# Moving the first fold of d K into the backward convolutions, and changing three loads, in an S4-gated SSM layer's forward and backward pass

## The chip, the cores and the metric

The kernel runs on one core of one Trainium2 chip. The metric is the device time in microseconds of one execution, from its first to its last instruction with what lies around them; lower is better. Five executions of the kernel before took 730.01, 740.09, 734.91, 728.99 and 732.19 us, so its median is 732.19 us.

## The reference, cut to what matters

The reference computes one layer and, by `jax.vjp`, its eleven gradients. All tensors are bf16; there are 2048 rows (time) of 512 channels, 128 states per channel, and a feed-forward network of width 1792.

```
xn  = layernorm(x)
K   = Re sum_n C[d,n] dB[d,n] exp(dt[d] A[d,n])**l       # the kernel of the convolution, per channel d
s   = causal convolution of xn with K along time + xn * Dskip
g   = silu( silu(xn @ w1) @ w2 )
out = x + s * g
and the gradients of out for x, A, B, C (real and imaginary), log_dt, Dskip, w1, w2
```

The backward pass first forms the gradient of `s` and of the network's output. The convolutions are done as Fourier transforms, so going back through them gives, per channel block, the gradient of xn through the convolution (dU) and the gradient of K (d K). From d K come the gradients of A, B, C and log_dt; "fold" is the first step on that way, which sums d K over groups of time steps. The gradient of x comes last, out of dU, the network's share and the layer norm.

## The kernel before, in words

Channels are cut into four blocks of 128, called b = 0 to 3; time rows are cut into eight chunks of two 128-row tiles, called c = 0 to 7. The parts of the work are Python generators that issue some instructions and then yield; helpers named `paced`, `woven` and `interleave` take turns among them. What comes out of that is not yet the order on the engines: the framework's scheduler arranges the issued instructions on each engine's queue when the kernel is built, with waits on semaphores between them. So the order on an engine is fixed at build time and can be read from the built kernel, and an instruction can stand before work that was issued earlier in the source.

The last part of `tile_recurrent_scan...` (L1132 to L1147) is the backward pass. Its stages:

1. **Backward convolutions**, about 300 to 465 us in the trace. `gen_conv_bwd` (L637) takes each block b through `forward(b)` (transform of the output gradient, lines L286, L297, L298, with its transposing DMAs L288) and `rest(b)`: a complex product on VectorE (L330 to L335), an inverse transform to d K (L310, then L319, cast by ScalarE at L44 and stored at L664), a second complex product, a second inverse transform to dU (L672, stored at L674). Beside it, at 1.8 steps to one, run `gen_ffn_da` (L867; matmuls L893 into ps_da and L904 into ps_dx, ScalarE's Silu and Tanh at L882 and L883, VectorE's L895) and `gen_out` (L607). `gen_out` makes the output: it loads rows of s, of the network's output (go_g) and of x (go_x, L626, one buffer), multiplies (L629), adds (L630) and stores with GpSimd's queue (L631). The load of x for a chunk is issued at the start of that chunk's own step.
2. **State gradients beside the rest of the network**, about 465 to 540 us. `gen_ssm_bwd` (L825) begins with six transposing loads of parameters (L346), then `ssm_fold` for b = 0: four loads of d K into the tile GE (L687), 23 short matmuls into one PSUM tile G21 (L703 and L705; the trace calls it G), and two casts by ScalarE into Gf (L706). Then come transposing loads of a table, YT (L725), VectorE's products Gb (L714), matmuls ps_v of YT and Gb (L736), ScalarE's casts Vb, VectorE's products Tp (L746), and sums by matmul (L758 to L762). The work runs in 16 groups of eight columns (L830), four to a block; the next block's fold is issued at the third group of a block.
3. **State gradients, gradients of w2 and w1, layer norm**, about 540 us to the end: `gen_dw2` (L911), `gen_dw1` (L943) and `gen_ln_bwd` (L961) take turns with the rest of `gen_ssm_bwd`. The layer norm loads dU, the network's share and rows of grad_out (Gt, L974, two buffers) and stores at L996.

Most loads and stores go through SyncE's queue (SP); a few go through ScalarE's, and the output stores through GpSimd's. The PSUM pool `pc` has two buffers; the transforms (ps_s, ps_i), the fold (G21) and ps_v all take theirs from it. The PSUM pool `pf` has three; the network's matmuls use it.

Of the kernel before, what the change touches and what calls it, by code (L numbers as in the profile page):

```python
# [13 lines left out]
BF16 = mybir.dt.bfloat16  # L14
# [3 lines left out]
P = 128  # L18
# [1 line left out]
PB = 18  # L20


BR, SR = 1.8, 0.5

E_EXP = [256 * i for i in range(1, 9)] + list(range(8)) + [258, 260, 262, 516, 772]
Y_EXP = [8 * j for j in range(1, 8)] + [64, 128, 192]
NE = len(E_EXP)
# [579 lines left out]
def gen_out(k, pool):  # L607

    nc = k.nc
    TT = nc.vector.tensor_tensor  # L610
    n = k.T // 2
    rows = lambda ap: ap.rearrange("p t (b d) -> p b t d", b=4)

    def load(c):
        ts = slice(2 * c, 2 * c + 2)
        S = pool.tile([P, 4, 2, P], BF16, name="go_s", tag="go_s", bufs=2)
        nc.sync.dma_start(S[:].rearrange("p b t d -> p b (t d)"), k.Sd[:, :, 256 * c:256 * c + 256].rearrange("b p n -> p b n"))
        g = pool.tile([P, 2, k.D], BF16, name="go_g", tag="go_g", bufs=2)
        nc.sync.dma_start(g[:], k.Od[:, ts, :])
        return S, g  # L620
    q = [load(0), load(1)]
    yield
    for c in range(n):
        S, g = q.pop(0)
        x = pool.tile([P, 2, k.D], BF16, name="go_x", tag="go_x", bufs=1)
        nc.sync.dma_start(x[:], k.x_v[:, 2 * c:2 * c + 2, :])  # L626
        nc.scalar.activation(out=g[:], in_=g[:], func=ACT.Silu)
        yield
        TT(out=rows(g[:]), in0=rows(g[:]), in1=S[:], op=ALU.mult)  # L629
        TT(out=x[:], in0=x[:], in1=g[:], op=ALU.add)  # L630
        k.st(k.o0_v[:, 2 * c:2 * c + 2, :], x[:])  # L631
        if c + 2 < n:
            q.append(load(c + 2))
        yield
# [47 lines left out]
def ssm_fold(k, b, sb):  # L682

    nc, pc = k.nc, k.pc
    GE = sb.tile([P, 8, 8, 32], BF16, name="GE", tag="GE", bufs=1)
    for a in range(4):
        nc.sync.dma_start(GE[a:P:4].rearrange("p i t q -> p i (t q)"), k.dKd[b, a].rearrange("i j r -> j i r"))  # L687
    G21 = pc.tile([P, 2, 512], F32, name="G21", tag="pc")
    ID, SH, WR, MX = 0, 1, 2, 3
    z0 = [(ID, GE[:, 0, 0:8, :], (0, 8, 16)), (ID, GE[:, 1:8, 0, :], (0, 0, 7)), (ID, GE[:, 1:8, 1, :], (0, 0, 7)),  # L690
          (ID, GE[:, 2:8, 2, :], (0, 1, 7)), (ID, GE[:, 4:8, 3, :], (0, 3, 7))]
    for st, e0 in ((SH, 0), (WR, 1)):
        z0 += [(st, GE[:, 1:8, 7, :], (0, e0, e0 + 7)), (st, GE[:, 2:8, 6, :], (0, e0 + 1, e0 + 7)),
               (st, GE[:, 4:8, 5, :], (0, e0 + 3, e0 + 7))]
    z0 += [(MX, GE[:, 4:8, 4, :], (0, 3, 7)), (WR, GE[:, 4:8, 4, :], (0, 4, 8))]
    z1 = [(ID, GE[:, 1, 2, :], (1, 0, 1)), (ID, GE[:, 1, 6, :], (1, 2, 3))]
    for t in (3, 4, 5):
        z1 += [(ID, GE[:, 1, t, :], (1, 1, 2)), (ID, GE[:, 2:4, t, :], (1, 3, 5))]
    Gf = sb.tile([P, 32, NE, 4], BF16, name="Gf", tag="Gf", bufs=2)
    for bank, terms in ((0, z0), (1, z1)):  # L700
        n = 16 if bank == 0 else 5
        ov = G21[:, bank, 0:32 * n].rearrange("p (e q) -> p e q", e=n)
        nc.tensor.matmul(out=G21[:, bank, 0:32 * n], lhsT=k.zero[:], rhs=GE[:].rearrange("p i t q -> p (i t q)")[:, 0:32 * n], start=True, stop=False)  # L703
        for i, (st, src, (bk, e0, e1)) in enumerate(terms):
            nc.tensor.matmul(out=ov[:, e0:e1], lhsT=k.FO[:, st], rhs=src, start=False, stop=(i == len(terms) - 1))  # L705
        nc.scalar.copy(out=Gf[:, :, 16 * bank:16 * bank + n, :],  # L706
                       in_=G21[:, bank, 0:32 * n].rearrange("p (e q) -> p q e", e=n).unsqueeze(3).to_broadcast([P, 32, n, 4]))
    return Gf
# [116 lines left out]
def gen_ssm_bwd(k, sb):  # L825


    par = load_params(k, sb, 0, k.D)
    par["dt"] = k.dt[:]
    groups = [(b, h, q0) for b in range(4) for h in range(2) for q0 in (0, 8)]  # L830
    gf, half, yt, vb, tp, S, tail = {}, {}, {}, {}, {}, {}, []
    gf[0] = ssm_fold(k, 0, sb)
    yt[0] = ssm_turned(k, *groups[0], sb)
    yield
    n = len(groups)
    for i in range(n + 2):
        if i < n:
            b, h, q0 = groups[i]
            if q0 == 0:
                half[i // 2] = ssm_half(k, b, h, gf[b], sb)  # L840
            if i + 1 < n:
                yt[i + 1] = ssm_turned(k, *groups[i + 1], sb)
            vb[i] = ssm_v(k, q0, half[i // 2][0], yt.pop(i), sb)
            if (i % 4) == 2 and b < 3:
                gf[b + 1] = ssm_fold(k, b + 1, sb)
            yield
        if i >= 2:
            j = i - 2
            b, h, q0 = groups[j]
            if (j % 4) == 0:  # L850
                S[b] = sb.tile([P, 3, 32, 2, 4], F32, name="Sa", tag="Sa", bufs=2)
            ssm_sums(k, tp.pop(j), S[b][:, :, 16 * h + q0:16 * h + q0 + 8])
            yield
            if (j % 4) == 3:
                tail.append(gen_ssm_grads(k, b, S.pop(b), par, sb))
        if 1 <= i <= n:
            tp[i - 1] = ssm_products(k, groups[i - 1][2], vb.pop(i - 1), half[(i - 1) // 2][1], sb)
            yield
        if tail:
            if next(tail[0], "end") == "end":  # L860
                tail.pop(0)
    for t in tail:
        yield from t
# [97 lines left out]
def gen_ln_bwd(k, lw):  # L961
    nc = k.nc
    TT, STT = nc.vector.tensor_tensor, nc.vector.scalar_tensor_tensor
    D = k.D
    n = k.T // 2
    cols = lambda ap: ap.rearrange("p (b d) -> p b d", b=4)

    def load(c):
        du = lw.tile([P, 4, 2, P], BF16, name="du", tag="du", bufs=3)
        nc.sync.dma_start(du[:].rearrange("p b t d -> p b (t d)"), k.dUd[:, :, 256 * c:256 * c + 256].rearrange("b p n -> p b n"))  # L970
        pd = lw.tile([P, 2, D], BF16, name="pd_l", tag="pd_l", bufs=3)
        nc.sync.dma_start(pd[:], k.Pd[:, 2 * c:2 * c + 2, :])
        Gt = lw.tile([P, 2, D], BF16, name="Gt", tag="Gt", bufs=2)
        nc.sync.dma_start(Gt[:], k.g_v[:, 2 * c:2 * c + 2, :])  # L974
        return du, pd, Gt

    def sums(c, du, pd, Gt):

        m = lw.tile([P, 2, 4], F32, name="m", tag="m", bufs=2)
        for i in range(2):  # L980
            t = 2 * c + i
            jk = lw.tile([P, D], BF16, name="jk", tag="jk", bufs=1)
            STT(out=cols(pd[:, i]), in0=cols(pd[:, i]), scalar=1.0, in1=du[:, :, i, :], op0=ALU.mult, op1=ALU.add, accum_out=m[:, i, 0:1])
            STT(out=jk[:], in0=pd[:, i], scalar=1.0, in1=k.xn[:, t, :], op0=ALU.mult, op1=ALU.mult, accum_out=m[:, i, 1:2])
        STT(out=m[:, :, 2:4], in0=m[:, :, 0:2], scalar=-1.0 / D,
            in1=k.rstd[:, 2 * c:2 * c + 2].unsqueeze(2).to_broadcast([P, 2, 2]), op0=ALU.mult, op1=ALU.mult)
        for i in range(2):
            nc.scalar.activation(out=pd[:, i], in_=pd[:, i], func=ACT.Identity, scale=k.rstd[:, 2 * c + i:2 * c + i + 1], bias=m[:, i, 2:3])
        return pd, Gt, m

    def rows(c, pd, Gt, m):
        o1 = lw.tile([P, 2, D], BF16, name="o1", tag="o1", bufs=2)
        for i in range(2):
            STT(out=o1[:, i], in0=k.xn[:, 2 * c + i, :], scalar=m[:, i, 3:4], in1=Gt[:, i], op0=ALU.mult, op1=ALU.add)
        TT(out=o1[:], in0=o1[:], in1=pd[:], op=ALU.add)
        k.st(k.o1_v[:, 2 * c:2 * c + 2, :], o1[:])  # L996
    q, pend = [load(0)], None
    for c in range(n + 1):
        if c + 1 < n:
            q.append(load(c + 1))  # L1000
        yield
        cur = sums(c, *q.pop(0)) if c < n else None
        yield
        if pend:
            rows(c - 1, *pend)
        pend = cur


@with_exitstack
def kernel(ctx, tc, A_u, A_A_re, A_A_im, A_B_re, A_B_im, A_C_re, A_C_im, A_log_dt, A_Dskip, B_x, B_w1, B_w2, grad_out,  # L1010
           out_0, out_1, out_2, out_3, out_4, out_5, out_6, out_7, out_8, out_9, out_10, out_11):
    nc = tc.nc
    k = KCtx()
# [115 lines left out]
    base = dft_pool("dftb", es_x, {"cm2": 1, "xd": 1, "w8b": 2}, k.dft, side="right")  # L1129
    turn = itertools.cycle(["w8"] * 4 + ["w8b"] * 2)  # L1130
    k.dftb = SimpleNamespace(tile=lambda shape, dt, name, tag: base.tile(shape, dt, name=name, tag=next(turn) if tag == "w8" else tag))
    da = pool("da", es=es_d)  # L1132
    turned_in_place(k, k.W2, k.evw)
    bwd = gen_conv_bwd(k)
# [1 line left out]
    for i in range(4):  # L1136
        next(bwd)
    ffb = gen_ffn_da(k, da)
    paced(bwd, woven([ffb, out], [2, 1]), BR)
    es_x.close()  # L1140
    sb = pool("sb", side="right")
    ssm = gen_ssm_bwd(k, sb)
    paced(ffb, ssm, SR)
    run(out)
    es_d.close()
    fw = pool("fw")
    interleave([ssm, chained([gen_dw2(k, fw), gen_dw1(k, fw)]), after(8, gen_ln_bwd(k, fw))], [2, 1, 2])  # L1147
# [1 line left out]
_INS = ['A_u', 'A_A_re', 'A_A_im', 'A_B_re', 'A_B_im', 'A_C_re', 'A_C_im', 'A_log_dt', 'A_Dskip', 'B_x', 'B_w1', 'B_w2', 'grad_out']  # L1149
# [26 lines left out]
```

## Time and profile before

| what | value |
| --- | --- |
| median of five executions | 732.19 us (728.99 to 740.09) |
| the profiled execution: its own time | 730.01 us |
| its span, first to last instruction | 728.3 us |
| mean granted TensorE clock | 0.946 |
| TensorE (PE) busy, modelled | 594.1 us, 82% of the span |
| VectorE (DVE) busy | 553.4 us, 76% |
| ScalarE (ACT) busy | 495.8 us, 68% |
| GpSimd (POOL) busy | 100.0 us, 14% |
| HBM traffic | 65.14 MB read, 62.26 MB written |
| DMA queue of SP and the other hardware queue q1 | 135.29 MB, 70.6% of 16 engines' span |

The busy time of an engine is a sum over stages with different limits; the stages around the change have to be read one by one. In the timeline a row has the start in us, the duration in us, the engine, the line of the source, the operation and its tiles, and, where the engine sat idle just before, for how long and what ended it. SPq marks an instruction of SP's queue that only issues a transfer, with the time it took to issue. In the list of waits a row says who waited for whom, then the total in us, how many times, and the longest.

### The profile page before, as it was taken

The numbers are of one execution on the slowest core, as the hardware profiler recorded it, in microseconds if no ns is written. First come the engines' busy times: TensorE is split into PE (matmuls) and PEld (weight loads), VectorE is DVE, ScalarE is ACT, GpSimd is POOL, SyncE is SP. The second block draws the span as 40 slices with busy tenths as digits, with TensorE's granted clock in tenths as the row PEclk, the third lists the DMA queues.
The fourth block names the chain that finished last, engine by engine and source line by source line (L and its number), as shares of the span: only waits on it lengthen the run. The fifth ranks groups of instructions, "written<-read, shape, count | busy, mean of one in ns | idle before, by whom it ended". The sixth has DMA issues, their size and how long they took to land.

```text
span 728.3 us, 13901 instructions
## 1 busy us (share of the span) xinstructions
PE 594.1 (82%) x5459; PEld 427.1 (59%) x5500; DVE 553.4 (76%) x1070; ACT 495.8 (68%) x671; POOL 100.0 (14%) x180
## 2 busy tenths in 40 slices
PE   0677868869999965569798899978797979898895
PEld 0445646555665743346576576757576656566784
DVE  6969997969978759976895999756896898784100
ACT  6768858779889866858779687646755867661221
POOL 2172200000010026200000000000002103102300
PEclk9879998999999995879999999999999989999998
DMA  9867957769679986579987965589979999920772
GB/s 288 310 164 204 256 175 210 283 154 294 286 195 247 364 268 162 185 170 257 319 211 238 247 216 198 153 218 210 227 161 283 249 300 276 233 106 27 160 183 59
DMA packets 207043, 159.26 MB, mean 219 GB/s; under 512 B 129025, under 2 KB 185345, under 8 KB 203393
## 3 DMA queue, kind: packets, MB, share of 16 engines
q1 hardware_dynamic: 193856, 135.29, 70.6%
q0 software_dynamic: 6224, 18.10, 6.8%
q10 hardware_dynamic: 6896, 4.98, 2.2%
q8 instruction: 43, 0.70, 0.4%
q14 instruction: 24, 0.19, 0.1%
HBM read 65.14 MB, written 62.26 MB: 175 GB/s over the span
## 4 chain that ended last, share of the span: by engine, by line
issue 53%; POOL 5%; DVE 5%; DMA 2%; PE 0%; ACT 0%; POOLq 0%; ACTq 0%; SPq 0%; DVEq 0%
POOL out_dram L816 1%; POOL out_dram L939 1%; DMA out_dram<-o 1%; DVE YD L599 1%; DMA Gr<-in_grad_out_dram 1%; DMA Kd<-KE 1%; DVE sp_in L332 1%; POOL out_dram L631 1%; DVE ds L595 1%; POOL out_dram L996 1%; POOL out_dram L958 1%; DVE sp_in L337 0%; POOL g L598 0%; DVE YD L603 0%; DVE YD L601 0%
## 5 line engine op out<-in xcount | busy, mean ns | idle before, releaser
L44 ACT CAST dA<-ps_s 128x1024 bf16<-128x1024 f32 x96 | 94.6, 1041 | 17.0 <-PE ps_s L298 8.5
L310 PE MATMUL ps_i<-I,sp_in 128*128 128x256 bf16 x384 | 54.3, 288 | 15.6 <-ACT dK L44 7.5
L893 PE MATMUL ps_da<-doT,W 128*128 128x256 bf16 x448 | 61.9, 284 | 5.5 <-ACT doT L44 2.9
L541 PE MATMUL ps_h<-XT,W 128*128 128x256 bf16 x448 | 62.4, 290 | 1.5 <-ACT hT L44 0.8
L44 ACT CAST o<-ps_w 128x256 bf16<-128x256 f32 (+1 forms) x42 | 18.6, 442 | 57.1 <-PE ps_w L954 42.4
L558 PE MATMUL ps_o<-W,aT 128*128 128x512 bf16 x209 | 54.5, 393 | 3.3 <-ACT aT L549 2.0
L44 ACT CAST dB<-ps_i 128x1024 bf16<-128x1024 f32 x48 | 47.2, 1024 | 14.6 <-PE ps_i L310 12.2
L310 PEld LDWEIGHTS <-sp_in 128*128 128x128 bf16 x384 | 37.4, 102 | 31.3 <-DVE sp_in L333 11.9
L746 DVE TENSOR_TENSOR Tp<-Vb,Eb 128x1344 bf16<-128x1344 bf16 x64 | 52.4, 855 | 3.7 <-PE psS L762 3.6
L893 PEld LDWEIGHTS <-W 128*128 128x128 bf16 x448 | 44.9, 102 | 16.3 <-issue 6.7
L904 PE MATMUL ps_dx<-W,dhT 128*128 128x512 bf16 x224 | 53.7, 379 | 0.0
L541 PEld LDWEIGHTS <-W 128*128 128x128 bf16 x448 | 45.6, 104 | 12.6 <-issue 2.5
L936 PE MATMUL ps_w<-YD,a_tok 128*128 128x512 bf16 x210 | 50.8, 387 | 2.5 <-ACT o L44 1.6
L954 PE MATMUL ps_w<-dh_tok,xn 128*128 128x256 bf16 x448 | 50.5, 273 | 2.4 <-DMA dh_tok<-DHd 2.0
L895 DVE SCALAR_TENSOR_TENSOR dhT<-dhT,ps_da 128x512 bf16<-128x512 bf16 x56 | 37.5, 684 | 14.7 <-PE ps_da L893 14.5
L954 PEld LDWEIGHTS <-xn 128*128 128x128 bf16 x448 | 43.2, 98 | 8.5 <-issue 3.6
L44 ACT CAST Vb<-ps_v 128x672 bf16<-128x672 f32 x64 | 42.5, 723 | 7.6 <-PE ps_v L736 7.6
L286 PEld LDWEIGHTS <-TF 128*128 128x128 bf16 x384 | 26.0, 101 | 26.9 <-issue 15.4
L419 ACT ACTIVATE sn<-V 128x1024 bf16<-128x1024 int32 (+3 forms) x40 | 34.8, 887 | 8.8 <-DVE V L417 8.8
L297 PE MATMUL ps_s<-dB,F 128*128 128x512 bf16 x87 | 34.3, 401 | 6.3 <-DMA dB<-dA 3.8
L298 PE MATMUL ps_s<-dB,F 128*128 128x512 bf16 x95 | 36.6, 390 | 2.7 <-DMA dB<-dA 2.0
L447 PEld LDWEIGHTS <-YD 128*128 128x128 bf16 x512 | 24.0, 100 | 23.2 <-DVE YD L434 12.1
(220 smaller groups left out, 1363.6 us busy)
## 6 DMA issues: line engine op xcount, KB each, us to landing
Yd<-YD SPq DMA_DIRECT2D x8, 1024.0 KB, 6.3
sp_in<-Ud SPq DMA_DIRECT2D x8, 1024.0 KB, 7.2
h_in<-Hd SPq DMA_DIRECT2D x14, 512.0 KB, 5.5
Ed<-E SPq DMA_DIRECT2D x8, 672.0 KB, 5.9
Eb<-Ed SPq DMA_DIRECT2D x8, 672.0 KB, 5.5
Hd<-hT POOLq DMA_DIRECT2D x8, 512.0 KB, 7.8
Ud<-dA SPq DMA_DIRECT2D x4, 1024.0 KB, 8.9
KXd<-dA SPq DMA_DIRECT2D x4, 1024.0 KB, 7.0
```

The lines of the kernel that those rows point to most:

```text
L44: return self.nc.scalar.copy(out=out, in_=in_)
L298: nc.tensor.matmul(out=ps[:, 4 * u:4 * u + 4], lhsT=F2[:, m1], rhs=B[:, 1, g0:g0 + 4, :], start=False, stop=True)
L310: nc.tensor.matmul(out=ps[:, g], lhsT=Y[:, c, g0 + g, :], rhs=k.I2[:, c].rearrange("p c m -> p (c m)"), start=(c == 0), stop=(c == 1))
L419: nc.scalar.activation(out=sn[:, :, 0:n], in_=V[:, :, 0:n], func=ACT.Sin, scale=-2 * PI_LO / 2.0 ** 32)
L541: nc.tensor.matmul(out=ps[:, j], lhsT=k.W1[:, dk, ft * P:ft * P + P], rhs=XTv[:, :, dk, :], start=(dk == 0), stop=(dk == DK - 1))
L558: nc.tensor.matmul(out=ps[:], lhsT=aT[:, ft, t * P:t * P + P], rhs=k.W2[:, ft, :], start=(ft == 0), stop=(ft == FT - 1))
L746: k.nc.vector.tensor_tensor(out=Tp[:, c, :, r ^ c].rearrange("p e (q w) a -> p q w e a", w=2), in0=Vb[:, :, c].rearrange("p q w (e a) -> p ...
L893: nc.tensor.matmul(out=ps[:, j], lhsT=k.W2[:, ft, dk * P:dk * P + P], rhs=dTv[:, :, dk, :], start=(dk == 0), stop=(dk == DK - 1))
L895: nc.vector.scalar_tensor_tensor(out=dh[:, i0:i0 + 2, :], in0=dh[:, i0:i0 + 2, :], scalar=1.0, in1=ps[:], op0=ALU.add, op1=ALU.mult)
L904: nc.tensor.matmul(out=ps[:], lhsT=dhs[ft // 8][:, ft % 8, t * P:t * P + P], rhs=k.W1[:, :, ft * P:ft * P + P], start=(ft == 0), stop=(ft ...
L936: nc.tensor.matmul(out=ps[:], lhsT=at[:, t, :], rhs=k.do[:, t, :], start=(t == 0), stop=(t == k.T - 1))
L954: nc.tensor.matmul(out=ps[:], lhsT=k.xn[:, t, dk * P:dk * P + P], rhs=dh[:, t].rearrange("p j n -> p (j n)"), start=(t == 0), stop=(t == k ...
```

## The change

Four edits:

- `ssm_fold` for b = 0 is no longer issued at the start of `gen_ssm_bwd`. A wrapper around `gen_conv_bwd` issues it when it has counted step 28 (FOLD) after the first four: that is in block b = 3, between the two halves of the inverse transform that gives d K of block 3. `gen_ssm_bwd` takes the result.
- Its tile GE comes then from the buffer "cm2" of the pool `dft`, which the backward convolutions do not use; Gf of even blocks comes from a new pool `sf`, later from `fw`, and Gf of odd blocks from `sb`, one buffer each instead of two in `sb`.
- In `gen_out` the load of x for chunk c + 1 is issued right after the store of chunk c, one yield earlier than before. The tile keeps its single buffer.
- In `gen_ln_bwd` two chunks are loaded at the start and the load of chunk c + 2 stands at the end of step c; Gt has three buffers instead of two.

```
-BR, SR = 1.8, 0.5
+BR, SR, FOLD = 1.8, 0.5, 28
...
+    def load_x(c):
+        x = pool.tile([P, 2, k.D], BF16, name="go_x", tag="go_x", bufs=1)
+        nc.sync.dma_start(x[:], k.x_v[:, 2 * c:2 * c + 2, :])
+        return x
     q = [load(0), load(1)]
+    x = load_x(0)
     yield
     for c in range(n):
         S, g = q.pop(0)
-        x = pool.tile([P, 2, k.D], BF16, name="go_x", tag="go_x", bufs=1)
-        nc.sync.dma_start(x[:], k.x_v[:, 2 * c:2 * c + 2, :])
...
         k.st(k.o0_v[:, 2 * c:2 * c + 2, :], x[:])
+        if c + 1 < n:
+            x = load_x(c + 1)
         if c + 2 < n:
             q.append(load(c + 2))
...
-    GE = sb.tile([P, 8, 8, 32], BF16, name="GE", tag="GE", bufs=1)
+    GE = sb.tile([P, 8, 8, 32], BF16, name="GE", tag="GE", bufs=1) if sb else k.dft.tile([P, 8, 8, 32], BF16, name="GE", tag="cm2")
...
-    Gf = sb.tile([P, 32, NE, 4], BF16, name="Gf", tag="Gf", bufs=2)
+    Gf = (sb if b % 2 else k.sf).tile([P, 32, NE, 4], BF16, name="Gf", tag="Gf", bufs=1)
...
-    gf[0] = ssm_fold(k, 0, sb)
+    gf[0] = k.gf0
...
-        Gt = lw.tile([P, 2, D], BF16, name="Gt", tag="Gt", bufs=2)
+        Gt = lw.tile([P, 2, D], BF16, name="Gt", tag="Gt", bufs=3)
...
-    q, pend = [load(0)], None
+    q, pend = [load(0), load(1)], None
     for c in range(n + 1):
-        if c + 1 < n:
-            q.append(load(c + 1))
         yield
...
         pend = cur
+        if c + 2 < n:
+            q.append(load(c + 2))
...
+    k.sf = pool("sf", es=es_d)
...
-    paced(bwd, woven([ffb, out], [2, 1]), BR)
+
+    def bwd_and_fold():
+        for i, _ in enumerate(bwd):
+            if i == FOLD:
+                k.gf0 = ssm_fold(k, 0, None)
+            yield
+    paced(bwd_and_fold(), woven([ffb, out], [2, 1]), BR)
...
-    fw = pool("fw")
+    fw = k.sf = pool("fw")
```

## The prediction

> **What bounds the kernel now.** I first read the busy times in short windows (columns: window, length, then busy time with instruction count of PE, PEld, DVE, ACT and POOL, granted clock, DMA share, GB/s). Two stages matter.
>
> ```profile
> 440.00:460.00 20.00, 18.91 (x168) 14.19 (x166) 19.43 (x30) 16.97 (x18) 0.89 (x1) 1.00 0.54 175
> 475.00:480.00 5.00, 3.75 (x21) 1.77 (x20) 2.73 (x5) 0.00 (x0) 0.00 (x0) 1.00 0.63 145
> 480.00:485.00 5.00, 4.96 (x40) 3.01 (x41) 0.42 (x1) 2.56 (x2) 0.00 (x0) 1.00 1.09 219
> ```
>
> Where the fold goes (440 to 460) PE and DVE are both nearly full. Where it stands now, DVE and ACT are almost empty for 10 us, but PE is not: it fills the hole with the network's matmuls. So the hole is worth only what PE loses in it. I read that from the waits by engine, 466 to 530 us:
>
> ```profile
> DVE Gb L714 <- ACT Gf L706: 11.6, 2, 6.8
> ...
> PE ps_da L893 <- ACT pd_s L44: 2.6, 2, 1.4
> ...
> PE ps_v L736 <- DMA YT<-Yd: 1.9, 3, 1.2
> PE G L703 <- DMA GE<-dKd: 1.3, 1, 1.3
> PE ps_da L893 <- ACT doT L44: 0.9, 1, 0.9
> PE ps_v L736 <- DVE Gb L714: 0.4, 1, 0.4
> ```
>
> DVE's longest wait is 6.8 us, PE's four around the first ps_v are 0.86 (doT), 1.27 (GE), 0.42 (Gb) and 1.18 (pd_s): 3.7 us. The timeline shows what they hang on:
>
> ```profile
> 472.97 1.26 SPq L346 DMA_TRANSPOSE par_Ci<-in_A_C_im_dram  x1
> 474.28 2.66 SPq L687 DMA_DIRECT2D GE<-dKd  x4
> 476.98 2.68 SPq L725 DMA_TRANSPOSE YT<-Yd  x2
> 480.02 0.38 PE L703 MATMUL G<-GE,zero 128*128 128x512 bf16 x1 [1.27 <-DMA GE<-dKd]
> 481.46 1.86 ACT L706 CAST Gf<-G 128x2048 bf16<-128x2048 f32 x1 [6.81 <-PE G L705]
> 484.58 3.03 DVE L714 TENSOR_TENSOR Gb<-Gf,MK 128x2688 bf16<-128x2688 bf16 x2 [6.78 <-ACT Gf L706]
> 486.19 0.74 PE L736 MATMUL ps_v<-Gb,YT 128*128 128x168 bf16 x8 [0.42 <-DVE Gb L714]
> ```
>
> SP's queue is one line: six parameter transposes (466.07 to 474.28, 8.2 us), four GE loads, then YT. PE's ps_v needs both Gb and YT. YT's transposes take long:
>
> ```profile
> DMA to landing us min/median/max: 3.8/5.5/8.9
> ```
>
> (4.97 listed as 5.0 between 460 and 500 us.) For the x rows I read VectorE's timeline:
>
> ```profile
> 363.60 0.68 DVE L331 TENSOR_TENSOR cm<-sp_in,dA 128x1024 bf16<-128x1024 bf16 x1
> 364.32 1.22 DVE L332 TENSOR_TENSOR sp_in<-sp_in,dA 128x2048 bf16<-128x2048 bf16 x1
> 400.21 0.69 DVE L630 TENSOR_TENSOR go_x<-go_x,go_g 128x1024 bf16<-128x1024 bf16 x1 [3.60 <-DMA go_x<-in_A_u_dram]
> ```
>
> DVE waits three times for x, 7.0 us in all (3.05, 0.33, 3.60).
>
> **What the Trainium skill says.** "DMA: Bandwidth & Descriptors", Anatomy of one DMA: a wait on a semaphore happens on the issuing sequencer, so a waiting load holds its queue. The trace agrees: SP waits for stores of x six times, 20.6 us. "PSUM — Partial Sum Buffer", Engine vs sequencer instructions: ScalarE and VectorE are strictly first in, first out, and matmuls start in program order; the trace shows PE idle 1.27 us at G with other matmuls behind it. "DMA: Bandwidth & Descriptors", Issuing engines are not separate DMA queues: all transfers share 16 engines; the DMA share of 1.09 at 480 to 485 us says that they are crowded there.
>
> **The change, part by part.** I compared the order of the two built kernels, engine by engine; a shift below is against before, positive is later.
>
> *x rows.* With one buffer, a load must still wait until the previous store has landed, so it is not really a chunk ahead. Chunk 3: x(2) is stored at 358.62, SP issues the load at 364.69 in both kernels, and x lands 3.2 us later (median of 330 to 440 us), 367.9. But the scheduler, which sees the load issued earlier, now puts the addition of chunk 3 right after the L331 that ends at 364.28, fourteen instructions before its old place at 374.86. DVE then stands 3.6 us where it had no wait, with L332, both L672 and the first L286 matmuls (which wait for a `pc` buffer freed by L672) behind it. Given back: go_g(5) is now loaded near 369, ahead of dU's store and two transposes, not at 378.95, so ACT's 4.62 us wait for it at 383.28 goes, and with it PE's 2.59 us wait for d K at 385.34. Moved fillers (four L904 fewer there) cost PE nothing. By 385 PE is level. Then the addition of chunk 4 comes at 388, before DVE's two L895, not at 390.44; its store lands 5.1 us and the next x 3.2 us later, 398 with issue, against 400.2. Two DVE instructions (1.3 us) that stood before the stall now stand behind it: 2.4 - 1.3 = 1.1 us gained. Sum **-1.1**; bounds +3.6 (nothing given back) and -3.6 (the stall at 400 gone for free).
>
> *The fold in block 3.* Four GE loads (0.6 us of SP each) move up to about 360 to 375, past the parameter loads, the last stores and the transposes of block 2. d K of block 0 was stored at 352.4, landing at most 8.5 us later, so they wait for nothing; SP behind them is late by 2.4 us plus the store of x(3): the L288 transposes go from 372.09 to about 377, land by 387 and are needed at 393.2. That cover of 6 us makes it zero. PE gets the fold's matmuls: 480.02 to 481.26 and 483.37 to 483.65, 1.5 us. ACT gets 1.86 + 0.69 = 2.55 us, in the order Tanh, Gf, d K, Gf, pd_s, Silu, d K. G holds one of two `pc` buffers meanwhile. Replayed on before's clock: G 445.8 to 447.1; the first 16 L319 to 448.0; ACT's Tanh to 448.2, Gf to 450.1; G's second part must wait for it (PE has matmuls to 449.5: 0.5 us idle); d K to 451.1, Gf to 451.8, which frees the buffer for the second 16 L319 (0.7 us idle); d K done at 455.3 against 450.55; then dB casts, and the last L319 starts at 462.4 against 459.96. Added: **+2.4**; bounds +1.5 (work alone) and +4.8 (the delay of d K in full).
>
> *The start of the state gradients.* Removed on PE: 1.5 us of fold and 3.7 us of waits. Gb moves into DVE's 3.58 us hole before 468.3, so it costs nothing there. But YT does not move up by as much as PE does. SP's six parameter loads still follow dU's last store (464.77), the last pd_s and one more slope load that now waits for L110: about 468.8, all at a shift of +2.4, so YT is issued at 468.8 + 8.2 = 477.0. PE meets the first ps_v after L118 and ten L893: 473.1 + 2.5 = 475.6. With 5.0 us to land YT comes at 482.0: 6.4 us idle, and the second half 1.3 us later with six L893 (0.7) between: +0.6. (x shifts PE and SP alike.) So 7.0 - 5.2 = **+1.8**. The wait changes its name from GE and pd_s to YT. Behind it on PE stand all the network's matmuls. YT at 2.5 us (as par_Ci landed) makes it -0.7, at 8.9 us +5.7.
>
> *After that.* DVE's first Tp starts near 485.5 instead of 490.60, so the state gradients lead the network's matmuls by 5 us more; some of PE's later waits on them (7.6 us for Vb, 1.5 at most once for gout) should shrink. I take **-1.5**, bounds 0 and -3.
>
> *Norm-gradient rows.* Load c + 2 at the end of step c stands where it stood, at the start of step c + 1, with no yield between. Only the third buffer is new: it takes SP's waits of 2.5, 0.4 and 0.3 us at Gt away. No engine waits for Gt; loads of h_in and YT behind it are covered by PE work. Zero, at best -2.5. Pools: the buffer of GE is idle then; zero.
>
> Sum: -1.1 + 2.4 + 1.8 - 1.5 = +1.6 us. The profiled execution took 730.0 (span 728.3, 1.7 around it), so 731.6; the median shown lies 2.2 above that execution, so I forecast 732.2 + 1.6 = **733.8**.
>
> **Rivals.** *Faster:* YT lands in 2.5 us (-0.7), the stall at 400 goes free (-3.6), the fold costs only its work (+1.5), the later lead is worth 3 PE's waits for YT at 494.93 and 496.17 go (-1.5), and SP's freedom at Gt is worth its 2.5: -9.8, **722.4**. For it: DVE's 6.8 us and 7.0 us of waits do exist. Against: PE hid most of them. *Slower:* one mechanism, PE held at the first ps_v (L736) until YT has landed. At the longest landing, 8.9 us, it costs +5.7, with the fold's +2.4 and no gain elsewhere +8.1: **740.3**. It passes +1% (7.3 us) from a landing of 8.1 us. For it: DMA share over 1 there; against: without GE's loads the crowd is thinner. *The loads do nothing:* the x rows and Gt change nothing, and the fold alone counts: +2.4 + 1.8 - 1.5, **734.9**.
>
> **How the numbers follow.** Stalls traded, my forecast: 0.52, own range 729 to 738. Loads do nothing: 0.16, the same verdict. Faster rival 0.13. Slower rival 0.19. Within 1% (about what a measurement can tell from no change, 724.9 to 739.5): 0.52 + 0.16 = 0.68; faster 0.13, slower 0.19. The range reaches from 726 to 742, to the upper half of the faster rival and past the slower one by half of the x stall's 3.6; about 0.1 lies outside on each side.
>
> **What would show it.** Right: a DVE wait of about 3.6 us at go_x near 365 and none near 400; G at about 446 with PE waits below 1 us; PE waiting for YT at the first L736 for 5 us or more, no wait at GE; first Tp earlier by 5 us than the network's matmuls beside it. Wrong: PE reaching L736 with YT landed; the L288 transposes of block 2 late for L297; waits for ps_i of over 3 us in block 3.

## The result and the profile after

The changed kernel took 738.02 us (median of 43 executions, 731.39 to 745.73), the kernel before on the same chips 733.74 us (80 executions). The ratio is 1.0056 with a 95% interval of 1.0040 to 1.0072: slower by 0.56%, or about 4.1 us. The profiled execution took 735.73 us, its span is 734.0 us, and the mean granted clock is 0.937.

The busy times in the same windows as before (window, length, then PE, PEld, DVE, ACT and POOL, granted clock, DMA share, GB/s):

```profile
440.00:460.00 20.00, 19.25 (x170) 13.81 (x168) 20.00 (x29) 15.41 (x17) 0.52 (x1) 1.00 0.52 172
475.00:480.00 5.00, 3.12 (x33) 2.60 (x30) 4.44 (x7) 4.31 (x3) 0.00 (x0) 1.00 0.62 123
480.00:485.00 5.00, 0.00 (x0) 0.00 (x0) 0.44 (x1) 0.41 (x1) 0.00 (x0) 0.61 0.82 97
```

The hole at 475 to 485 is filled on VectorE and ScalarE for its first half, and then the engines stand: VectorE and ScalarE work 0.44 and 0.41 us of the 5 from 480 to 485, and PE, which had been busy for 4.96 of them, does nothing. The waits between 466 and 530 us (total, times, longest) say for what:

```profile
PE ps_v L742 <- DMA YT<-Yd: 8.2, 2, 7.0
...
DVE Gb L720 <- ACT Gf L712: 4.4, 1, 4.4
...
PE ps_da L899 <- ACT pd_s L44: 0.7, 1, 0.7
...
PE G L709 <- ACT Gf L712: 0.3, 1, 0.3
PE ps_da L899 <- ACT doT L44: 0.3, 1, 0.3
```

VectorE's 11.6 us for Gb have become 4.4, and PE's wait for GE is gone. In exchange PE waits 8.2 us for YT (1.9 before). The timeline has the chain, which starts at SP's queue:

```profile
470.23 1.55 DVE L720 TENSOR_TENSOR Gb<-Gf,MK 128x2688 bf16<-128x2688 bf16 x1
...
478.30 1.26 SPq L346 DMA_TRANSPOSE par_Ci<-in_A_C_im_dram  x1
...
479.60 2.67 SPq L731 DMA_TRANSPOSE YT<-Yd  x2
...
485.09 0.46 PE L742 MATMUL ps_v<-Gb,YT 128*128 128x168 bf16 x2 [6.96 <-DMA YT<-Yd]
```

The first half of Gb is ready at 471.8, YT is issued at 479.6 and PE runs at 485.1. The hole has a second price, to which the forecast gave no term. The column of the granted clock, in windows of 2 us:

```profile
480.00:482.00 2.00, 0.00 (x0) 0.00 (x0) 0.44 (x1) 0.41 (x1) 0.00 (x0) 0.77 0.58 96
...
484.00:486.00 2.00, 0.91 (x6) 0.73 (x7) 0.00 (x0) 0.00 (x0) 0.00 (x0) 0.50 0.83 154
486.00:488.00 2.00, 2.00 (x13) 1.69 (x12) 0.69 (x1) 0.71 (x2) 0.00 (x0) 0.53 1.07 357
488.00:490.00 2.00, 2.00 (x20) 1.46 (x17) 0.95 (x2) 1.91 (x4) 0.00 (x0) 1.00 0.92 229
```

Some 3 us into PE's idle stretch the clock falls to one half, and it stays there until about 487.9, 2.8 us after PE has begun again: 13 matmuls in 2 us, then 20. My estimate from these lines is 1.4 us of PE's work lost on top of the wait. In the kernel before the clock is 1.00 in all these windows.

For the x rows VectorE's timeline shows two stalls where one was:

```profile
370.04 0.69 DVE L634 TENSOR_TENSOR go_x<-go_x,go_g 128x1024 bf16<-128x1024 bf16 x1 [3.23 <-DMA go_x<-in_A_u_dram]
...
402.57 0.69 DVE L634 TENSOR_TENSOR go_x<-go_x,go_g 128x1024 bf16<-128x1024 bf16 x1 [5.74 <-DMA go_x<-in_A_u_dram]
```

In all VectorE waits 11.0 us for x (7.0 before).

To see in which stage the time went, I took six landmarks from the timelines: the Silu of chunk 3's rows in `gen_out` (360.07 in the kernel before), the stores of dU of block 2 (440.33) and block 3 (464.77), the state sums Sa of the fifth and the last of the 16 groups (543.87, 664.93), and the last store (720.90). The table gives, for each profiled execution, how much longer each stretch took than in the kernel before. The experiments are told below.

| kernel | to 360 | blocks 0 to 2 | block 3 (the fold) | 465 to 544 | 544 to 665 | rest |
| --- | --- | --- | --- | --- | --- | --- |
| changed kernel | +2.54 | +1.02 | +0.87 | -0.34 | +1.59 | +0.03 |
| fold alone | +1.86 | +3.79 | +0.87 | 0.00 | +4.47 | -0.45 |
| fold and x | +2.10 | +0.47 | +0.87 | +0.20 | +3.32 | -0.15 |
| changed, GE on GpSimd | +3.00 | +2.45 | +0.87 | -1.20 | +3.31 | +2.99 |
| changed, YT(0) first | +0.64 | +1.45 | +0.87 | -0.26 | +0.54 | -1.52 |
| changed, parameters in step 4 | +2.36 | +2.59 | +0.88 | -2.53 | +2.42 | +0.68 |
| changed, parameters in step 1 | +3.83 | +1.51 | +1.54 | +0.67 | +1.17 | -0.46 |
| changed, GE on GpSimd and parameters in step 1 | -3.11 | +0.50 | +1.49 | +0.51 | +3.87 | -0.56 |
| x alone | +2.70 | -0.47 | -0.12 | +0.27 | -2.91 | +4.68 |
| Gt alone | +1.34 | -0.81 | -0.12 | +2.55 | +7.60 | +0.47 |
| Gt in place | +1.98 | +0.11 | +0.05 | +1.57 | -0.99 | -0.02 |

Three things say how far such a table can be trusted. Up to 360 us all these kernels have the same order of instructions on PE, VectorE and ScalarE, and yet their profiled executions stand from 3.1 us earlier to 3.8 us later there than that of before; ten of eleven are later, so the profile of before was an early one, and the change has no part in that. And the kernel with x alone has the order of before on all four compute engines to the end, yet its last two columns are off by -2.9 and +4.7. And five of the kernels have the same order on every engine and on SP's queue from the start to 465 us (the changed kernel, fold and x, YT(0) first, parameters in step 1 and in step 4), and their blocks 0 to 2 are longer by anything from 0.47 to 2.59 us. So a stage of 80 us or more is known to 2 or 3 us from one profile. The column of block 3 is much finer: +0.87 or +0.88 in six of the eight rows with the fold and 1.5 in the other two, -0.12 to +0.05 in the three without. The profiled executions of the last two experiments were slow ones, 1.6% above the fastest of their kernels, so they are not in the table.

### The profile page after: what moved, and what is told of

Read it like the earlier page. It is cut to its first block, busy times and chain, and to the rows that moved or that the text cites. A ratio compares the mean times of both kernels' runs of the same rounds, so it can differ in the third digit from the quotient of the medians.

```text
span 734.0 us, 13897 instructions
## 1 busy us (share of the span) xinstructions
PE 595.2 (81%) x5459; PEld 431.1 (59%) x5500; DVE 553.9 (75%) x1070; ACT 496.9 (68%) x671; POOL 100.8 (14%) x180
## 4 chain that ended last, share of the span: by engine, by line
issue 49%; DVE 7%; POOL 4%; DMA 3%; PE 2%; ACT 1%; POOLq 0%; SPq 0%; DVEq 0%; ACTq 0%
DMA out_dram<-o 1%; PE ps_w L942 1%; DMA Gr<-in_grad_out_dram 1%; DVE YD L599 1%; POOL out_dram L822 1%; POOL out_dram L635 1%; DVE sp_in L332 1%; DVE ds L595 1%; POOL out_dram L945 1%; POOL out_dram L964 1%; DVE sp_in L333 0%; DMA pd_l<-Pd 0%; POOL out_dram L1002 0%; POOL g L598 0%; DVE YD L603 0%
## 5 line engine op out<-in xcount | busy, mean ns | idle before, releaser
L899 PE MATMUL ps_da<-doT,W 128*128 128x256 bf16 x448 | 59.8, 280 | 7.0 <-DVE dhT L901 4.1
L899 PEld LDWEIGHTS <-W 128*128 128x128 bf16 x448 | 44.5, 101 | 17.3 <-issue 8.4
L910 PE MATMUL ps_dx<-W,dhT 128*128 128x512 bf16 x224 | 54.1, 379 | 0.4 <-DVE dhT L901 0.3
L297 PE MATMUL ps_s<-dB,F 128*128 128x512 bf16 x87 | 34.0, 398 | 7.3 <-DMA dB<-dA 4.5
L742 PE MATMUL ps_v<-Gb,YT 128*128 128x168 bf16 x256 | 28.6, 242 | 11.6 <-DMA YT<-Yd 8.2
```

The costliest lines, as they stand in the source:

```text
L297: nc.tensor.matmul(out=ps[:, 4 * u:4 * u + 4], lhsT=F2[:, m0], rhs=B[:, 0, g0:g0 + 4, :], start=True, stop=False)
L899: nc.tensor.matmul(out=ps[:, j], lhsT=k.W2[:, ft, dk * P:dk * P + P], rhs=dTv[:, :, dk, :], start=(dk == 0), stop=(dk == DK - 1))
L910: nc.tensor.matmul(out=ps[:], lhsT=dhs[ft // 8][:, ft % 8, t * P:t * P + P], rhs=k.W1[:, :, ft * P:ft * P + P], start=(ft == 0), stop=(ft ...
```

## The experiments

### One edit at a time

The fold alone (loads of x and of Gt as before):

```
-        if c + 1 < n:
-            x = load_x(c + 1)
+        x = pool.tile([P, 2, k.D], BF16, name="go_x", tag="go_x", bufs=1)
+        nc.sync.dma_start(x[:], k.x_v[:, 2 * c:2 * c + 2, :])
...
-        Gt = lw.tile([P, 2, D], BF16, name="Gt", tag="Gt", bufs=3)
+        Gt = lw.tile([P, 2, D], BF16, name="Gt", tag="Gt", bufs=2)
```

> The changed kernel with the loads of x and of the norm-gradient rows as before; only the fold is moved. Theory (two separate losses: a later standing of VectorE for x, and a trade of waits at the start of the state gradients): the waits for x return to the 7.0 us of before, the wait of PE for YT at the first ps_v stays at 6 to 7 us, and the time is +0 to +2 us against before. Rival A (the fold alone is the loss): +4 us, as the whole change. Rival B (the last stage's load order is the loss): below +1 us, with landmarks of the state gradients level with before from 530 us on.

Measured: 1.0102 of before (1.0075 to 1.0129), more than the whole change. VectorE's waits for x, which I expected back at 7.0 us, are the longest of all:

```profile
DVE go_x L630 <- DMA go_x<-in_A_u_dram: 14.9, 4, 6.4
```

and the stall near 370 us, which I had put down to the early load of x, is there without it (the timeline):

```profile
371.06 0.69 DVE L630 TENSOR_TENSOR go_x<-go_x,go_g 128x1024 bf16<-128x1024 bf16 x1 [4.92 <-DMA go_x<-in_A_u_dram]
```

So this theory, and the step of my prediction behind it, falls: the stall comes with the fold. (This run and the one with Gt alone have six executions each, so their intervals are wide.)

The early load of x alone:

```
-        x = pool.tile([P, 2, k.D], BF16, name="go_x", tag="go_x", bufs=1)
-        nc.sync.dma_start(x[:], k.x_v[:, 2 * c:2 * c + 2, :])
...
         k.st(k.o0_v[:, 2 * c:2 * c + 2, :], x[:])
+        if c + 1 < n:
+            x = load_x(c + 1)
```

> The kernel before with only the load of x issued a yield earlier. Theory: VectorE waits for x about 11 us in three places (3 near 370 and 5 to 6 near 400) instead of 7.0, dU of block 1 is stored 2 to 4 us later than before, and the time is +2 to +4 us. Rival A (the fold alone is the loss): within 1 us of before. My prediction's own step for x said -1.1 us, with no wait for x left near 400.

Measured: 1.0026 (1.0002 to 1.0050), with less waiting for x than in the kernel before, and chunk 3's addition at its old place without a wait (waits, then timeline):

```profile
DVE go_x L634 <- DMA go_x<-in_A_u_dram: 4.4, 2, 2.8
```

```profile
377.56 0.68 DVE L634 TENSOR_TENSOR go_x<-go_x,go_g 128x1024 bf16<-128x1024 bf16 x1
```

The theory that x is a loss of its own is wrong as well: this edit moves nothing but two loads of x on SP, by one place each. Its 0.26% is at the edge of what the interval can tell from nothing.

The norm-gradient rows alone:

```
-        Gt = lw.tile([P, 2, D], BF16, name="Gt", tag="Gt", bufs=2)
+        Gt = lw.tile([P, 2, D], BF16, name="Gt", tag="Gt", bufs=3)
```

> The kernel before with only the norm-gradient rows in three buffers and loaded two chunks ahead. Theory and prediction: 0 us (from -1 to +1), since no engine waits for Gt. Rival B (the order of loads in the last stage makes the loss): +1.5 us or more, with longer waits for h_in or YT after 530 us.

Measured: 1.0104 (1.0071 to 1.0136), and +7.6 us in the last stage. I had costed this edit at nothing. Of its two parts only the third buffer counts: with the loads moved and two buffers the built kernel has the order of before on every engine (no run shows this). The third buffer leaves PE, ScalarE and GpSimd as they were, leaves VectorE as it was up to 623 us, and moves some lines of SP's queue. Where the time goes is seen at L994 for the third chunk, first in the kernel before and then in this one (SP's, GpSimd's and VectorE's timelines):

```profile
571.29 0.54 POOL L996 DMA_DIRECT2D out_dram<-o  x1 [2.02 <-DVE o L995]
571.90 5.71 SPq L725 DMA_TRANSPOSE YT<-Yd  x2
...
577.13 1.42 DVE L994 SCALAR_TENSOR_TENSOR o<-xn,m,Gt 128x512 bf16<-128x512 bf16 x2 [2.29 <-issue]
```

```profile
574.12 7.82 SPq L725 DMA_TRANSPOSE YT<-Yd  x2
575.27 0.54 POOL L996 DMA_DIRECT2D out_dram<-o  x1 [2.51 <-DVE o L995]
...
584.87 1.41 DVE L994 SCALAR_TENSOR_TENSOR o<-xn,m,Gt 128x512 bf16<-128x512 bf16 x2 [6.05 <-issue]
```

L994 writes into one of the two buffers o1, so it has to wait for the store of the first chunk. In the kernel before that store was issued 0.61 us ahead of a pair of transposing loads of YT, and was done 5.8 us later, at 577.04. Here it is issued 1.15 us behind the first of that pair, and takes 9.5 us, to 584.78; VectorE goes on within 0.1 us of either landing. SP's wait of 2.5 us for a buffer of Gt ahead of these loads is gone; what else brought YT ahead of the store was not taken apart.

The three edits run alone cost 1.02, 0.26 and 1.04%, which would make 2.3%; together they cost 0.56%. So they cannot be added up.

### Is the wait for YT the price of the fold?

YT's first two transposes ahead of the six parameter transposes:

```
+    yt[0] = ssm_turned(k, *groups[0], sb)
     par = load_params(k, sb, 0, k.D)
```

> The changed kernel with the first two transposing loads of YT issued ahead of the six parameter transposes, 8 us earlier on SP's queue. If PE's 7.0 us wait for YT at the first ps_v is the price of the moved fold, it is gone or below 1.5 us and the time falls by 4 to 6 us against the changed kernel, to about level with before or 2 us below it. If the hole only moves (VectorE or ScalarE late next, or the state gradients no longer on the path), the wait goes but the time falls by less than 2 us.

Measured: 1.0076 (1.0037 to 1.0115), no better than the changed kernel. PE's wait has only moved to the second YT, which now stands behind the parameters:

```profile
475.36 0.32 PE L742 MATMUL ps_v<-Gb,YT 128*128 128x168 bf16 x2 [1.40 <-DMA YT<-Yd]
...
487.90 0.46 PE L742 MATMUL ps_v<-Gb,YT 128*128 128x168 bf16 x2 [5.88 <-DMA YT<-Yd]
```

With the parameters issued one step later:

```
+        if i == 1:
+            par = load_params(k, sb, 0, k.D)
```

> The changed kernel with the six parameter transposes issued after the first group's step, so that both the first and the second YT stand ahead of them. With YT(0) alone ahead, the wait moved from the first YT (7.0 us) to the second (5.9 us). If SP's 8 us of parameter transposes are the price of the moved fold, PE's waits for YT between 466 and 530 us fall from 8.2 to below 3 us and the time falls by 3 to 6 us against the changed kernel. If the state gradients' start is not what the end follows from, the waits go but the time falls by less than 1.5 us.

Measured: 1.0064 (1.0033 to 1.0094). Now it is the third YT:

```profile
496.21 0.46 PE L742 MATMUL ps_v<-Gb,YT 128*128 128x168 bf16 x2 [6.76 <-DMA YT<-Yd]
```

And with them in step 4, behind five YT (`if i == 4`):

> The changed kernel with the six parameter transposes issued in the fifth step of the state gradients, behind five YT loads. With them ahead of the first, second or third YT the wait stood at that YT each time (7.0, 5.9, 6.8 us). If SP's 8 us of issuing have to be paid by PE wherever they stand among the YT loads, PE's waits for YT between 466 and 530 us stay at 7 us or more in all, and the time stays at 1.004 to 1.007 of before. If PE has cover later (network matmuls that no longer depend on YT), the waits fall below 4 us in all, and the time falls by 3 us or more against the changed kernel, to 1.002 or less. If the start of the state gradients does not set the end, the waits fall and the time stays.

Here most of the wait goes (waits 466 to 530 us), the clock stays at 1.00 until 520 us, and the stretch from 465 to 544 us is 2.2 us shorter than in the changed kernel:

```profile
PE ps_v L742 <- DMA YT<-Yd: 3.4, 5, 1.5
```

But the time is 1.0056 (1.0027 to 1.0086), that of the changed kernel. In this profile a later wait has grown: at the place where PE stands 3.51 us for VectorE's ddt in the changed kernel (618.64) it stands for twice as long.

```profile
619.67 0.48 PE L764 MATMUL psS<-Tp,ident 128*128 128x128 bf16 x3 [7.06 <-DVE ddt L826]
```

So the 7 us hole is the price of six transposes of 1.26 us on SP's queue when they stand ahead of the first, second or third YT, and it goes when they stand behind five. But closing it is worth nothing that the medians show. The gain of 3 us or more that I had named did not come, and of the three outcomes the third fits best: the start of the state gradients does not set the end. A gain of 2 us would be hidden in the interval.

### Is it the GE loads among the loads of x?

Fold and x together, Gt as before:

```
-        Gt = lw.tile([P, 2, D], BF16, name="Gt", tag="Gt", bufs=3)
+        Gt = lw.tile([P, 2, D], BF16, name="Gt", tag="Gt", bufs=2)
```

> The changed kernel with only the norm-gradient rows as before (two buffers): fold and early x. All engines but SP have the same order as in the changed kernel and as in the run with the fold alone, so the time tells what x and the third buffer are worth beside the fold (fold alone 1.0102, whole change 1.0056 of before). If the early x makes the difference: 1.005 or 1.006. If the third buffer makes it: 1.009 to 1.011.

Measured: 1.0089 (1.0052 to 1.0125). This lies between the two forecasts and its interval holds both, so it does not tell which of the two edits mends part of the fold's loss.

The first fold's four loads on GpSimd's queue:

```
-        nc.sync.dma_start(GE[a:P:4].rearrange("p i t q -> p i (t q)"), k.dKd[b, a].rearrange("i j r -> j i r"))
+        (nc.sync if sb else nc.gpsimd).dma_start(GE[a:P:4].rearrange("p i t q -> p i (t q)"), k.dKd[b, a].rearrange("i j r -> j i r"))
```

> The changed kernel with the four GE loads of the first fold on GpSimd's queue instead of SP's. New theory: these loads, standing on SP among the loads of x and the stores of dU near 360 to 377, are what moved the addition of chunk 3 ahead and what made the waits for x longer; without them the waits of VectorE for x are 5 us or less (11.0 in the changed kernel, 14.9 with the fold alone), block 0's dU is stored at most 2 us later than before, and the time falls by 3 to 4 us against the changed kernel, to 1.000 to 1.002 of before. My prediction (the early x moved it): the wait near 370 stays at 3 us and the time within 1 us of the changed kernel. Rival (the fold's own work in block 3 is the loss): also within 1 us.

Measured: 1.0046 (1.0020 to 1.0073), 0.1% below the changed kernel and not to be told from it. The cause of the stall near 370 is right: chunk 3's addition is back behind L335 and waits for nothing, and PE, VectorE and ScalarE have the order of before until the fold's own matmuls.

```profile
377.86 0.68 DVE L634 TENSOR_TENSOR go_x<-go_x,go_g 128x1024 bf16<-128x1024 bf16 x1
```

Block 0's dU is stored no later than in the kernel before, against 3.9 us later in the changed kernel (both beyond the shift that they had at 360 us). But by 410 us the changed kernel has made up for most of that: reckoned in the same way it is 1.0 us late there (3.56 less 2.54), and this one 1.3. The 3 to 4 us that I expected to win back were not there to be won. The wait at the sixth chunk stays: 7.4 us for x in all instead of 11.0, where I had named 5 or less. The time fits the rival as well, that the loss is the fold's own work; this run does not exclude it.

Both mends together:

> Both of the former: GE's first loads on GpSimd's queue and the parameters after the second YT. If the two losses are separate and both theories hold, the gains add: 6 to 9 us below the changed kernel, 0.993 to 0.997 of before, better than both kernels. If one of them holds, 3 to 5 us below the changed kernel, about level with before. If neither, level with the changed kernel (1.005).

Measured: 1.0053 (1.0031 to 1.0075), level with the changed kernel: the case "neither".

### The buffers of the layer norm's result

In the kernel before with the third Gt buffer, the result written into Gt's own tile:

```
-        o1 = lw.tile([P, 2, D], BF16, name="o1", tag="o1", bufs=2)
-            STT(out=o1[:, i], in0=k.xn[:, 2 * c + i, :], scalar=m[:, i, 3:4], in1=Gt[:, i], op0=ALU.mult, op1=ALU.add)
+            STT(out=Gt[:, i], in0=k.xn[:, 2 * c + i, :], scalar=m[:, i, 3:4], in1=Gt[:, i], op0=ALU.mult, op1=ALU.add)
...
-        Gt = lw.tile([P, 2, D], BF16, name="Gt", tag="Gt", bufs=3)
+        Gt = lw.tile([P, 2, D], BF16, name="Gt", tag="Gt", bufs=5)
```

> The kernel before with the norm-gradient rows two chunks ahead, and the layer norm's result written into Gt's own tile (five buffers) instead of into the two buffers o1; same memory as the run with Gt alone, which took 1.0104 of before. There VectorE stood 6.05 us at L994 for a buffer of o1 whose store landed 9.6 us after issue, against 2.3 us and 5.3 us in the kernel before. If that wait is the price of the third buffer, it is gone (0 at L994) and the time falls by 3 us or more, to 1.006 or less. If the loss comes from the changed order of SP's loads (YT and h_in against GE), the wait at L994 goes but the time stays near 1.010.

Measured: 0.9977 (0.9954 to 0.9999). The 1.04% are gone, and perhaps a little more: of the versions tried this is the only one whose interval lies below the kernel before, and it ends at 0.9999. The same store is again issued behind the first YT (574.20 and 573.30) and takes 10.1 us, but now nobody waits for it. SP's order is that of the run with the third buffer alone up to 597 us (five loads stand elsewhere after that), so at the place of the loss it is the wait that the edit took away, and not the order. VectorE's busy time from 570 to 590 us shows it, first with the third buffer alone (1.0104), then in place:

```profile
570.00:590.00 20.00, 18.44 (x198) 13.57 (x199) 13.92 (x31) 15.03 (x22) 3.27 (x6) 1.00 1.11 260
```

```profile
570.00:590.00 20.00, 17.52 (x193) 12.96 (x191) 19.75 (x53) 14.21 (x21) 3.28 (x6) 1.00 1.11 270
```

VectorE works 19.75 of 20 us instead of 13.92, at the same DMA share of 1.11. (In the kernel before it is 17.68. The 5.3 us that the expectation gives for the store is the median of such stores in the kernel before; the one that VectorE waited for took 5.8.)

The same in the changed kernel, and then with every mend at once (GE on GpSimd's queue, parameters in step 4, result in place):

> The changed kernel with the layer norm's result written into Gt's tile (five buffers, no o1), nothing else. In the kernel before with the third buffer alone this took the loss away (1.0104 to 0.9977). In the changed kernel VectorE's wait at L1000 is only 1.7 us. If the wait for o1 is also what the changed kernel loses in its last stage, the time falls by 3 us or more, to 1.001 or less. If its loss lies in the backward convolutions and the fold (about 1 us at each place) and the last stage has none of it, the time stays at 1.004 to 1.006.

> The changed kernel with GE's first loads on GpSimd's queue, the parameters in the fifth step, and the layer norm's result in Gt's tile. Every wait found so far is mended. If the moved fold pays once its side effects are gone, it is 0.995 or less, below the in-place version without the fold (0.9977). If the move is worth nothing in itself, because PE had work in the hole that it fills, it is level with that version, 0.997 to 1.000. If the fold costs by its own work in the full stretch, 1.002 or more.

Measured: 1.0033 (1.0010 to 1.0056) and 1.0022 (0.9991 to 1.0053). Writing in place is worth about 0.2% to the changed kernel, which the intervals don't separate from nothing, and not the 1.3% that it is worth where the wait for o1 was 6 us. The changed kernel's own wait there is short:

```profile
580.74 1.42 DVE L1000 SCALAR_TENSOR_TENSOR o<-xn,m,Gt 128x512 bf16<-128x512 bf16 x2 [1.68 <-issue]
```

Both forecasts for it, "1.001 or less" and "1.004 to 1.006", are missed. With everything mended the kernel is still 0.45% (half width about 0.4%) above the in-place version without the fold. By number that is the last of the three cases that I had named, the fold that costs by its own work; its interval reaches into the second, a move that is worth nothing.

## Why the prediction was right or wrong

The forecast was 733.8 us against a median of 732.2, so +1.6 us or 0.2%, within 1%. The measured ratio is +0.56%: the sign is right and the change is within 1%, and the size is low by about 2.5 us. Part of that nearness is luck. With the stages of the table (the changed kernel's +5.7 us of span less the 2.5 from before 360 us are +3.2), the x rows came out 2.1 us worse than forecast and the fold 1.5 us better, which nearly cancel; the start of the state gradients with what follows was 0.6 us better, and from 544 us on, where nothing was forecast, it took 1.6. Step by step:

- **x rows: predicted -1.1, measured +1.0 for blocks 0 to 2 (0.5 to 2.6 in the five profiles of the same order). This is the step that failed**, in two ways. First the cause. I read from the built order that chunk 3's addition moves ahead of L332, and wrote that the scheduler does so because it "sees the load issued earlier". The stall came as forecast (3.23 us for 3.6), but the run with the fold alone has it (4.92 us) and that with x alone has not: it is the four GE loads, put on SP between the loads of x at 362 to 376 us, that changed VectorE's order, for with these loads on GpSimd's queue the old order is back. I had put GE's loads at zero, from their effect on the L288 transposes alone. (That they "wait for nothing" was not so either: SP stands 1.4 us at one of them for d K.) Second the giving back. The chain was level soon after 385, as I said (the first row of d K of block 1 is stored at 387.49 for 385.72, 0.8 us early once the 2.5 are taken off), but the stall at 400 did not vanish; it grew to 5.74 us, because the load of x behind chunk 4's store was issued 7.8 us after the store, at 399.44, where I had counted 5.1 us of landing.
- **The fold in block 3: predicted +2.4, measured +0.87.** The order was as replayed, but PE's wait for Gf was 0.24 us instead of 0.5 and 0.7: other matmuls (L910, L899) stood in both gaps. My lower bound, +1.5 for the work alone, was too high too. Between the stores of dU of blocks 2 and 3 PE is busy for 24.77 of 25.30 us where it had been for 23.35 of 24.44: the work is 1.4 us more, and 0.6 us of it went into idle time.
- **The start of the state gradients: predicted +1.8, then -1.5.** The mechanism was as forecast. YT is issued at 479.60, which is 477.1 once the 2.5 us from before 360 are taken off (predicted 477.0), and lands after 5.4 us (predicted 5.0); PE waits 6.96 us at the first ps_v (predicted 6.4), and not at all at the second half (0.6), for the six L899 between take 1.3 us at half clock instead of 0.7; 1.20 us more come at a later YT. The half clock itself, about 1.4 us, was in no term. The first Tp starts at 490.25 with 481 of the network's 672 matmuls ahead of it, where 524 were before: a lead of 43 matmuls, 7 us by their mean of 0.17 us in the kernel before (predicted 5 us). The stretch from 465 to 544 us took -0.3 against the +0.3 of my two terms.
- **Norm-gradient rows: predicted 0; the sum does not hold that.** By itself the third buffer costs 1.0%. My reason, that no engine waits for Gt, was true and did not answer the question: with SP's loads in other places a YT load goes ahead of the store of o1 instead of behind it, and that store, for which VectorE waits, landed 9.5 us after issue instead of 5.8. In the changed kernel the same buffer did not cost that: there the store is issued ahead of YT (575.57 and 576.18), lands after 5.1 us, and VectorE stands 1.7 us.
- **Rivals.** *Slower*, with PE held for YT until 8.9 us after its issue, did not come: 5.4 us. *Faster* needed YT in 2.5 us and the stall at 400 free. *The loads do nothing* (734.9) is nearest in number, but each of its two loads does something: x alone takes the waits for x from 7.0 to 4.4 us, and Gt alone costs 1.0%.

What stays open is where the rest of the loss lies. With all the waits that I found mended, the moved fold (with the early x) still costs 0.45% against the in-place version, about 3.3 us and nearly as much either way; the early x alone was measured at 0.26%, so what is left for the fold itself is not told from nothing. In the table the eight kernels with the fold are longer by 0.5 to 3.8 us in blocks 0 to 2 and by 0.9 to 1.5 in block 3, and those without it by at most 0.1 in either. But the work in block 3 was only moved. From 360 to 544 us, with the stage included from which it was taken away, those with the fold are longer by 0.9 to 4.7 us and those without it by -0.3 to 1.7, which one profile each does not separate. In blocks 0 to 2 the order of the engines does not explain it: the two kernels of the table with GE on GpSimd's queue have the order of before there on PE, VectorE and ScalarE, and are longer by 2.45 and 0.50 us. The clock is an untested rival: against the kernel before beside it, its mean over all executions is 0.4% higher in the in-place version and level with everything mended. That PE filled the old hole with the network's matmuls, so that there was little to win, agrees with the runs in which the new hole was closed and the time stayed.

## What to carry to other kernels

Cost a moved step for every queue that its instructions land on, and compare the built order with one edit made at a time, not only with all: that alone would have told that the stall near 370 belonged to the fold and not to x. A hole on one engine is worth what the engine that sets the end loses in it; here a 7 us hole on PE could be closed with no change that the medians show. And a larger buffer is not free because nobody waits for it: ask how it shifts the loads of its queue, and which store then comes behind them.

## What was not expected of the hardware

A store of 256 KB took 5.8 us from issue to landing in one kernel and 9.5 us in the next, with the same work beside it in another order. In ten of the twelve profiles (the table's eleven and that of before) this store, the layer norm's first, is issued ahead of the pair of transposing loads of YT next to it, or at most 0.1 us behind the first of the two, and lands after 4.6 to 6.0 us. In the other two it is issued 0.9 and 1.2 us behind, and lands after 10.1 and 9.5 us. Why is not shown.

PE's clock fell to one half some 3 us into a 7 us idle stretch and stayed there for 2.8 us of the work behind it. With the parameters in step 4 there is no such stretch at that place, and the clock is 1.00 from 478 to 488 us.

The Trainium skill, "DMA: Bandwidth & Descriptors", Issuing engines are not separate DMA queues, says that issuing from several engines saves only the time on the sequencer, usually small beside the transfer. The run with GE's loads on GpSimd is in line with that (0.1%, within the noise). For transposes the issuing was not small: the six parameters held SP for 1.26 us each, 7.9 us in all, and landed 2.6 to 4.4 us after issue.
